# Reordering the head of a fused FFT and maxout feed-forward kernel

## The chip, the cores and the metric

The kernel runs on one core of one Trainium2 chip. The metric is the device time of one execution in microseconds (us), as the median over runs. A profiled execution also has a span, from its first to its last profiled instruction; the span is a little shorter than that execution's own time.

## The reference

The input x is 8 batches of 3072 rows by 256 columns. Each batch gets a two-dimensional Fourier transform, of which only the real part is kept. Then a feed-forward layer with three weight matrices and a maximum runs over all 24576 rows.

```python
def _attn_ref(x):
    X = np.fft.fft(x, axis=1)
    X = np.fft.fft(X, axis=2)
    return X.real.astype(np.float32)

def _moe_ref(x, w1, w2, w3, w_out):            # d_model 256, d_ff 768
    h = np.maximum(np.maximum(x @ w1, x @ w2), x @ w3)
    return (h @ w_out).astype(np.float32)
```

## The kernel before

**The work.** The transform over the 256 columns is folded into the weights. The kernel multiplies a cosine table `md` (and its negative `nmd`) with the differences of the weights and keeps the results as `g_all`, six blocks of 128 columns of the hidden layer; `gd_all` holds, scaled by one number per partition, those halves of `g_all` that belong to the odd part. `g1t` and `gw` are further products of the weights. What is left per batch is the transform over 3072 rows, in two steps, into an even part `tE` and an odd part `tO`, each 128 x 1536, and then the feed-forward layer on them. By symmetry each matmul pair gives a row k and its mirror 3072 - k: `hp` is the hidden layer of the one, `hm` of the other.

**Units.** A batch has 18 units: three blocks of 512 columns of `tE` and `tO`, times six blocks of the hidden layer. The loop over units at the end of the kernel writes the order of the work out by hand, and each engine executes in that order. A unit is `begin` (the plus matmuls L490 and L491, a relu on ACT into `stmp` L503, a maximum on DVE into `hp` L504) and, one unit later, `finish` (the minus matmuls L497 onto the same banks, the same relu and maximum into `hm`). From unit 7 on, every second unit takes its third term in another way (L814 to L844). The output matmuls of a block (L513, L536) are spread over the six units behind it.

**The head.** Everything ahead of the unit loop prepares batch 0. This report calls it the head, and units 0 to 5 the first block.

- GpSimd (POOL) makes index ramps (`iota`, L150), issues the loads of x (L127, four chunks of slots in two halves each) and of the weights (`load_w`, L173, in columns 0 to 128, 128 to 384 and 384 to 768), and later the loads of batch 1.
- DVE makes small per-partition numbers (`scal` L213, `mad` L217), the angles `vm` and `kvec`, and the mirrored half of each chunk of x (`mirror` L134); the mirrored first column goes to ACT or DVE (L138).
- PE multiplies each chunk with a table (`Mix.s`, L401 and L411, s(0) to s(6)), with matmuls on zeros in between (`warm_up`, L640). ACT or DVE copies the result from PSUM to `tb` (L408, L416). DVE transposes `tb` to `yb` in one instruction (`Mix.t`, L434), and `Mix.k` (L466) multiplies `yb` with the tables `te_tab` and `to_tab` that ACT makes (`table`, L302 to L306). `k(0, g)` gives block g of `tE`, `k(1, g)` block g of `tO`.
- `products` (L314) multiplies tables and weights into a PSUM bank, and `keep` (L328) copies the bank to `g_all`; `psg0` is hidden block 0, `psg1` and `psg2` are the two parts of blocks 1 and 2. `differ` (L335) makes `gd_all` from `g_all`.

**PSUM.** The head has two rings of banks: `ps_f`, three banks that last through the whole kernel, and `ps_s`, five banks that are closed ahead of the unit loop. The space of `ps_s` then becomes the banks of the units (`pse2`, `pse3`, `po`).

**Work placed among the units.** `plan` lists what batch 0 does behind `begin` of each unit: `m.c` (copies single columns into `yb`, L459), `m.f` (fills the edge rows of `yb`, L438 and L440), `m.k` for the later blocks, `angle` and `table` for the last third of the angles, and the generators `prep_first` (four pieces for hidden blocks 3 to 5, L314 and L344) and `prep_second` (`g1t`, L370 and L374; then `gw`, L379 and L384).

Of the kernel before, what the change touches and what calls it, by code (L numbers as in the profile page):

```python
# [51 lines left out]
def kernel(  # L52
# [9 lines left out]
    nc = tc.nc  # L62
# [9 lines left out]
    RI = 17  # L72
# [6 lines left out]
    ps_f = ctx.enter_context(tc.tile_pool(name="ps_f", bufs=3, space=bass.MemoryType.PSUM))  # L79
# [8 lines left out]
    tbw = tb.rearrange("p (f s) -> p f s", s=32)  # L88
# [56 lines left out]
    gen = ctx.enter_context(tc.tile_pool(name="gen", bufs=1))  # L145
    ps_s_cm = tc.tile_pool(name="ps_s", bufs=5, space=bass.MemoryType.PSUM)
    ps_s = ps_s_cm.__enter__()

    def iota(t, pattern, base=0, cm=0):
        nc.gpsimd.iota(t, pattern, base=base, channel_multiplier=cm,  # L150
                       allow_small_or_imprecise_dtypes=True)
# [2 lines left out]

    pidx = gen.tile([128, 1], FP32, tag="pidx")
    iota(pidx, [[0, 1]], cm=1)
    NA = 32 + 2 * RI
    ang_r = gen.tile([128, NA], FP32, tag="ang_r")
    iota(ang_r[:, 0:32], [[0, 2], [1, 16]], base=1)
# [11 lines left out]
    def load_w(k, j0, j1):  # L171
        wsrc, wdst = ((moe_w1, w1_bf), (moe_w2, w2_bf), (moe_w3, w3_bf))[k]
        nc.gpsimd.dma_start(  # L173
            out=wdst.rearrange("p (fc j) -> p fc j", fc=2)[:, :, j0:j1],
            in_=wsrc.rearrange("(fc p) j -> p fc j", fc=2)[:, :, j0:j1])
# [10 lines left out]
    load_w(1, 0, 128)  # L186
    ramp(6)
    load_w(2, 0, 128)
    for k in range(3):
        load_w(k, 128, 384)  # L190
    ramp(11)
# [10 lines left out]
    nc.vector.memset(half_pi, 0.5 * math.pi)  # L202
    ang_o = gen.tile([128, NA], FP32, tag="ang_o")
    nc.vector.memset(ang_o, 0.0)
    nc.vector.memset(ang_o[:, 15:32], 8.0)
    nc.vector.memset(ang_o[:, NA - RI:NA], 24.0)
    nc.vector.memset(ang_r[:, 31:32], 0.0)
# [23 lines left out]
    mad(ang_r, ang_r, alpha, ang_o)  # L231
    _reduce(nc, ang_r, ang_r, ang_q, 32.0)
    nc.scalar.activation(out=ang_q, in_=ang_r, func=AX.Sin, scale=float(2.0 * math.pi / 32.0))
    half = gen.tile([128, 256], FP32, tag="half")
    nc.vector.memset(half[:, 0:128], 64.0)
    nc.vector.memset(half[:, 128:256], 0.0)
    par = gen.tile([128, 2], FP32, tag="par")
    scal(par[:, 1:2], pidx, 0.5, ALU.mult, -0.25, ALU.add)
    scal(par[:, 1:2], par[:, 1:2], ROUND, ALU.add)
    scal(par[:, 1:2], par[:, 1:2], -ROUND, ALU.add, -2.0, ALU.mult)  # L240
    nc.vector.tensor_tensor(out=par[:, 1:2], in0=par[:, 1:2], in1=pidx, op=ALU.add)
    scal(par[:, 1:2], par[:, 1:2], 64.0, ALU.mult)
    scal(par[:, 0:1], par[:, 1:2], -1.0, ALU.mult, 64.0, ALU.add)
    nc.vector.tensor_copy(out=tab[:, 0:64:2], in_=ang_q[:, 0:32])
    scal(tab[:, 1:64:2], ang_q[:, 0:32], sig, ALU.mult)
    scal(tabx, ang_q[:, 32:NA], sgm, ALU.mult)
# [2 lines left out]
    vm = gen.tile([128, 512], FP32, tag="vm")  # L249
    qm = gen.tile([128, 512], FP32, tag="qm")  # L250
    pf = gen.tile([128, 2], FP32, tag="pf")
    rnd = gen.tile([128, 2], FP32, tag="rnd")
    for fc in range(2):
        scal(pf[:, fc:fc + 1], pidx, float(128 * fc), ALU.add)
        nc.vector.scalar_tensor_tensor(
            out=vm[:, fc * 256:(fc + 1) * 256].rearrange("p (k c) -> p k c", c=128),
            in0=dvec.unsqueeze(1).to_broadcast([128, 2, 128]), scalar=pf[:, fc:fc + 1],
            in1=half.rearrange("p (k c) -> p k c", c=128), op0=ALU.mult, op1=ALU.add)
    nc.vector.memset(rnd[:, 0:1], ROUND)
    nc.vector.memset(rnd[:, 1:2], -ROUND)  # L260

    def turns(q, v, per):

# [20 lines left out]
    mad(vm, qm, -256.0, vm)  # L284
    nc.vector.tensor_copy(out=vm.rearrange("p (fc k c) -> p fc k c", fc=2, k=2)[:, :, :, 0],
                          in_=par.unsqueeze(1).to_broadcast([128, 2, 2]))
    nc.vector.memset(tbw[:, :, 24:32], 0)
    mirror(0, *FIRST[1])

    def angle(part, c0=1024, c1=NHALF + 1):  # L290
        cs = slice(c0, c1)
        if part == 0:
            phase(c0, c1)
            scal(q[:, cs], kvec[:, cs], 1.0 / 3072.0, ALU.mult, ROUND, ALU.add)
        else:
            scal(q[:, cs], q[:, cs], -ROUND, ALU.add, -3072.0, ALU.mult)
            nc.vector.tensor_tensor(out=kvec[:, cs], in0=kvec[:, cs], in1=q[:, cs], op=ALU.add)

    def table(k, c0=1024, c1=NHALF + 1):
# [18 lines left out]
    def products(pool, i0, i1, j0, j1, tag="ps"):  # L318

        psg = pool.tile([128, 512], FP32, name="psg", tag=tag)  # L320
        for i in range(i0, i1):
            for half in range(2):
                product(psg, (2 * (i - i0) + half) * (j1 - j0), i, half, j0, j1)
        return psg

    def keep(psg, i0, i1, j0, j1, evict):

        evict(out=g_all[:, j0 // 128:j1 // 128, 2 * i0:2 * i1, :],  # L328
              in_=psg[:, 0:2 * (i1 - i0) * (j1 - j0)].rearrange("p (k c j) -> p c k j", j=128,
                                                               c=(j1 - j0) // 128))  # L330

    def differ(i0, i1, j0, j1):

        cs = slice(j0 // 128, j1 // 128)
        nc.vector.tensor_scalar(out=gd_all[:, cs, i0:i1, :], in0=g_all[:, cs, 2 * i0 + 1:2 * i1:2, :],  # L335
                                scalar1=dif, scalar2=None, op0=ALU.mult)
# [51 lines left out]
    class Mix:  # L388
# [46 lines left out]

        def f(self):
            for a in (0, 64):
                nc.scalar.copy(out=ybv[a + 32:a + 64, 0], in_=ybv[a:a + 32, 16])  # L438
                for r in (0, 32):
                    nc.vector.memset(ybw[a:a + 32, r:r + 2, :], 0)  # L440

        def col(self, slot, which):
            return ybv[:, (slot + 1) % RI, which, :]
# [194 lines left out]
    def warm_up(n):  # L638
        for _ in range(n):
            nc.tensor.matmul(warm, zero[:, 0:128], zero, start=True, stop=True)  # L640

    m = Mix(0)
    warm_up(17)
    m.s(0, pool=ps_s)
    m.s(1, pool=ps_s)
    warm_up(5)
    wrap(0, 512)
    mirror(0, *FIRST[2])
    nc.scalar.activation(out=md_all, in_=vm, func=AX.Sin, scale=float(2.0 * math.pi / 256.0))
    m.s(2, pool=ps_s)  # L650
    m.s(3, pool=ps_s)
    phase(512, 1024)
    mirror(0, *FIRST[3])
    m.s(4, pool=ps_s)
    scal(sgn, pidx, 0.0, ALU.is_equal)
    scal(sgn, sgn, 2.0, ALU.mult, -1.0, ALU.add)
    m.s(5, pool=ps_s, evict=dve)
    m.s(6, pool=ps_s)
    m.t()
    nc.scalar.activation(out=nmd_all, in_=vm, func=AX.Sin, scale=float(-2.0 * math.pi / 256.0))  # L660
    table(0, 0, 512)
    table(1, 0, 512)
    table(2, 0, 512)
    for k in range(3):
        load_w(k, 384, 768)
    m.u()
# [9 lines left out]
                                in_=moe_w_out.rearrange("(jc p) c -> p jc c", jc=NJC))  # L676
    psg0 = products(ps_f, 0, 2, 0, 128)
    keep(psg0, 0, 2, 0, 128, nc.scalar.copy)
    psg1 = products(ps_s, 0, 1, 128, 384)
    m.x0(x0s)  # L680
    warm_up(2)
    m.c(1, 7)
    m.k(0, 0, dve)
    m.k(1, 0)
    psg2 = products(ps_s, 1, 2, 128, 384)
    wrap(512, 1024)
    keep(psg1, 0, 1, 128, 384, dve)
    scal(dif, sgn, 1.0, ALU.subtract)
    differ(0, 2, 0, 128)
    keep(psg2, 1, 2, 128, 384, dve)  # L690
    table(1, 512, 1024)

    rows_f = gen.tile([128, 12 * B], FP32, tag="rows_f")
    iota(rows_f.rearrange("p (b t u) -> p b t u", t=4, u=3), [[S, B], [-4, 4], [-1025, 3]],
# [5 lines left out]
    pool = nc.gpsimd  # L700
# [60 lines left out]
        mirror(b, *EIGHTHS[ch])  # L761

    for (u, fn) in ((0, lambda: table(2, 512, 1024)), (0, lambda: m.c(7, 16)),
                    (0, lambda: next(second)), (0, lambda: differ(0, 2, 128, 384)),
                    (1, lambda: table(0, 512, 1024)), (2, m.f), (2, lambda: m.c(0, 1)),
                    (2, lambda: m.c(16, RI)),
                    (1, lambda: m.k(1, 1)), (1, lambda: next(second)), (1, lambda: angle(0)),
                    (2, lambda: m.v(1)), (2, lambda: m.k(0, 1)),
                    (2, lambda: next(first)), (2, lambda: next(first)), (2, lambda: next(second)),
                    (2, lambda: next(first)), (2, lambda: next(first)), (2, lambda: angle(1)),  # L770
                    (3, lambda: table(1)), (3, lambda: table(2)), (3, lambda: table(0)),
                    (4, lambda: m.k(1, 2)), (4, lambda: m.k(0, 2)), (4, m.end),
                    (5, column), (5, lambda: next(second)), (6, lambda: m.v(2))):
        at(0, u, fn)
# [145 lines left out]
```

## Time and profile before

| | |
|---|---|
| median of 3 runs | 403.43 us (403.2 to 405.6) |
| profiled execution, own time | 403.34 us |
| its span | 401.5 us |
| mean granted TensorE clock | 0.989 |
| PE matmul busy | 383.7 us (96%), 2755 matmuls |
| DVE busy | 321.0 us (80%), 542 instructions |
| ACT busy | 262.6 us (65%), 476 instructions |
| POOL busy | 329.9 us (82%), 422 instructions |
| HBM read and written | 36.95 MB and 30.81 MB |

An engine's busy time is the time in which it has an instruction under way. A busy share over the whole span is a mean over stages; the head and the first block, some 43 us, differ from the other 350 us. The granted clock is the share of full speed that TensorE runs at. A line of a timeline has the start in us, the duration, the engine, the line of the kernel and the tiles; in brackets the idle time of the engine ahead of it, and what ended it.

### The profile page before, as it was taken

How to read it: one execution, taken by the hardware profiler on the slowest of the kernel's cores; microseconds unless marked ns; L12 is line 12 of the kernel's file. 1: busy time of each engine (PE TensorE's matmuls, PEld its weight loads, DVE VectorE, ACT ScalarE, POOL GpSimd, SP SyncE). 2: the span in 40 equal slices, each digit the busy share in tenths (PEclk: the TensorE clock that was granted, in tenths of full speed). 3: DMA queues.
4: the chain of work that ended last, by engine and by line, in shares of the span. 5: the costliest groups of instructions: out<-in, count | busy, mean ns of one | idle time of the engine just before them, and what ended most of it. 6: DMA issues, size and time to landing. Idle time of an engine off the chain costs nothing.

```text
span 401.5 us, 8422 instructions
## 1 busy us (share of the span) xinstructions
PE 383.7 (96%) x2755; PEld 237.7 (59%) x2755; DVE 321.0 (80%) x542; ACT 262.6 (65%) x476; POOL 329.9 (82%) x422
## 2 busy tenths in 40 slices
PE   6777999999999999999999999999999999999994
PEld 2443555656665566656665666656665666666673
DVE  7877796877887887877887887877887887887982
ACT  3857678768875778668865778568866546544420
POOL 9991279788998899888998899898978798778993
PEclk9799999999999999999999999999999999999999
DMA  8999259386766958495665968396332653322234
GB/s 115 165 182 175 42 141 196 104 149 182 156 127 132 201 133 154 124 170 157 159 147 111 194 145 165 107 183 169 105 107 83 142 144 100 93 74 53 89 90 133
DMA packets 66901, 54.20 MB, mean 135 GB/s; under 512 B 32702, under 2 KB 62556, under 8 KB 66003
## 3 DMA queue, kind: packets, MB, share of 16 engines
q0 software_dynamic: 24368, 26.53, 35.1%
q1 hardware_dynamic: 41978, 26.72, 26.3%
q8 instruction: 21, 0.34, 0.4%
q10 hardware_dynamic: 512, 0.43, 0.4%
q14 instruction: 22, 0.18, 0.2%
HBM read 36.95 MB, written 30.81 MB: 169 GB/s over the span
## 4 chain that ended last, share of the span: by engine, by line
PE 89%; DVE 5%; ACT 3%; issue 1%; DVEq 0%; ACTq 0%
PE po L513 31%; PE pse L497 12%; PE pse L490 8%; PE pse L491 8%; PE po L536 5%; PE pse L830 4%; PE pse L831 4%; PE e L814 4%; PE d L816 4%; PE ps L401 3%; PE ps L466 3%; PE pl L528 2%; PE psg L314 1%; ACT stmp L503 1%; DVE hp L504 1%
## 5 line engine op out<-in xcount | busy, mean ns | idle before, releaser
L503 ACT ACTIVATE stmp<-pse 128x512 bf16<-128x512 f32 x150 | 89.6, 600 | 66.2 <-PE pse L497 42.0
L823 POOL TENSOR_TENSOR plus<-even,odd 128x512 bf16<-128x512 f32 x69 | 87.8, 1272 | 44.6 <-DVE even L819 27.9
L622 POOL DMA_INDIRECT out_dram<-ot,rows_m x92 | 102.3, 1112 | 17.8 <-issue 9.5
L823 POOL TENSOR_TENSOR minus<-even,odd 128x512 bf16<-128x512 f32 x69 | 87.5, 1269 | 0.0
L513 PE MATMUL po<-wout_bf,hp 128*128 128x256 bf16 x576 | 86.1, 273 | 0.0
L832 DVE SCALAR_TENSOR_TENSOR hp<-pse,plus 128x512 bf16<-128x512 f32 x69 | 47.6, 690 | 43.7 <-PE pse L831 25.2
L513 PE MATMUL po<-wout_bf,hm 128*128 128x256 bf16 x576 | 78.6, 273 | 0.0
L513 PEld LDWEIGHTS <-hp 128*128 128x128 bf16 x576 | 56.3, 98 | 26.1
L497 PE MATMUL pse<-tO,gd_all 128*128 128x512 bf16 x219 | 70.8, 379 | 0.0
L513 PEld LDWEIGHTS <-hm 128*128 128x128 bf16 x576 | 56.4, 98 | 16.3
L541 DVE TENSOR_TENSOR ot<-po,even 128x512 f32<-128x512 f32 x92 | 62.8, 683 | 0.0
L490 PE MATMUL pse<-tE,g_all 128*128 128x512 bf16 x150 | 56.8, 379 | 4.5 <-DVE hm L504 2.1
L504 DVE TENSOR_TENSOR hp<-pse,stmp 128x512 bf16<-128x512 f32 x75 | 51.4, 686 | 10.4 <-ACT stmp L503 9.8
L504 DVE TENSOR_TENSOR hm<-pse,stmp 128x512 bf16<-128x512 f32 x75 | 51.6, 688 | 9.0 <-ACT stmp L503 3.7
L491 PE MATMUL pse<-tO,g_all 128*128 128x512 bf16 x150 | 56.8, 379 | 0.0
L819 DVE SCALAR_TENSOR_TENSOR even<-vb,wcol,e 128x512 f32<-128x512 bf16 x69 | 50.9, 738 | 0.0
L844 DVE SCALAR_TENSOR_TENSOR hm<-pse,minus 128x512 bf16<-128x512 f32 x69 | 47.2, 684 | 2.1 <-PE pse L491 1.5
L818 ACT ACTIVATE odd<-d 128x512 f32<-128x512 f32 x69 | 41.3, 599 | 6.0
L134 ACT COPY xt<-xt 64x762 bf16<-64x762 bf16 (+1 forms) x48 | 40.2, 838 | 1.1
L536 PE MATMUL po<-gw,tO 128*128 128x512 bf16 x92 | 34.9, 380 | 0.0
L497 PEld LDWEIGHTS <-gd_all 128*128 128x128 bf16 x219 | 21.3, 97 | 23.1 <-issue 5.0
L405 ACT CAST tb<-ps 128x512 bf16<-128x512 f32 x40 | 21.6, 588 | 14.8 <-PE ps L401 14.0
(177 smaller groups left out, 488.9 us busy)
## 6 DMA issues: line engine op xcount, KB each, us to landing
xt<-in_x_dram POOLq DMA_DIRECT2D x14, 384.0 KB
out_dram<-ot SPq DMA_DIRECT2D x55, 96.0 KB
out_dram<-ot SPq DMA_DIRECT2D x64, 64.0 KB
db<-tb SPq DMA_DIRECT2D x21, 192.0 KB
vb<-vd SPq DMA_DIRECT2D x23, 128.0 KB
xt<-in_x_dram POOLq DMA_DIRECT2D x7, 400.0 KB
xt<-in_x_dram POOLq DMA_DIRECT2D x7, 368.0 KB
out_dram<-ot SPq DMA_DIRECT2D x62, 32.0 KB
```

The costliest lines, as they stand in the source:

```text
L490: nc.tensor.matmul(pse[:, 0:n], g_all[:, jc, 2 * i, :], te, start=True, stop=False)
L491: nc.tensor.matmul(pse[:, 0:n], g_all[:, jc, 2 * i + 1, :], to, start=False, stop=True)
L497: nc.tensor.matmul(pse, gd_all[:, jc, i, :], to, start=False, stop=True, skip_group_check=True)
L503: nc.scalar.activation(out=stmp[:, 0:n], in_=pses[0][:, 0:n], func=AX.Relu)
L504: nc.vector.tensor_tensor(out=dst, in0=src3, in1=stmp[:, 0:n], op=ALU.max)
L513: nc.tensor.matmul(po, hcols(jc), wout_bf[:, jc * 256:(jc + 1) * 256], start=False, stop=(jc == NJC - 1), skip_group_check=True)
L536: nc.tensor.matmul(po, to[:, cp], gw[:, 256:768], start=True, stop=True)
L541: nc.vector.tensor_tensor(out=ot.rearrange("p (h c) -> p h c", h=2), in0=po.rearrange("p (h c) -> p h c", h=2), in1=lin.unsqueeze(1).to_br ...
L622: stored(nc.gpsimd.indirect_dma_start(out, bass.IndirectOffsetOnAxis(ap=rows_m[0:128 - lo, at_row: at_row + 1], axis=0), ot[lo:128, 256:51 ...
L819: nc.vector.scalar_tensor_tensor(out=even3, in0=vb, scalar=wcol[:, jc:jc + 1], in1=e3, op0=ALU.mult, op1=ALU.add)
L823: nc.gpsimd.tensor_tensor(out=dst, in0=even3, in1=odd3, op=op)
L832: nc.vector.scalar_tensor_tensor(out=dst, in0=pse2, scalar=0.0, in1=sums[g][0], op0=ALU.max, op1=ALU.max)
```

## The change

It touches the head and the plan of units 0 to 3 of batch 0. The rest of the kernel is the same text.

- Small numbers on DVE: the parity of the partition (`par`) comes from an integer ramp and a bit operation, three instructions in place of six; the tile `half` and its two memsets go, and `vm` is made by four `tensor_scalar` in place of two `scalar_tensor_tensor`; the two memsets of `rnd` move to the front. One `iota` is added on POOL ahead of the loads.
- The memset of the spare slots of `tb` moves from DVE to POOL, between two loads of weights.
- `phase(512, 1024)` moves on DVE from behind the third mirror to ahead of the second.
- s(3) is copied by DVE in place of ACT, s(5) by ACT in place of DVE, s(6) by DVE in place of ACT.
- Fillers: 18 + 4 + 1 + 2 + 2 + 3 = 30 matmuls on zeros in place of 17 + 5 + 2 = 24.
- `psg1` and `psg2` go from the ring `ps_s` to the ring `ps_f`; `psg1` is copied by ACT ahead of `m.k`, in place of DVE behind it. ACT makes `table(1)` and `table(2)` behind the copy of `psg0`.
- `differ(0, 2, 128, 384)` and `m.f` move from units 0 and 2 into the head, and `m.f` from ACT and DVE to POOL, ahead of the row numbers (`rows_f`) and of POOL's mirrors of batch 1.
- The plan: one piece of `prep_first` goes behind unit 0 and one behind unit 1, two stay at unit 2 (before, all four were there); `table(0, 512, 1024)` comes later in unit 1; the last two `m.c` go to unit 3.

```diff
     iota(pidx, [[0, 1]], cm=1)
+    pidx_i = gen.tile([128, 1], INT32, tag="pidx_i")
+    nc.gpsimd.iota(pidx_i, [[0, 1]], base=0, channel_multiplier=1)
...
     load_w(2, 0, 128)
+    nc.gpsimd.memset(tbw[:, :, 24:32], 0)
     for k in range(3):
         load_w(k, 128, 384)
...
+    rnd = gen.tile([128, 2], FP32, tag="rnd")
+    nc.vector.memset(rnd[:, 0:1], ROUND)
+    nc.vector.memset(rnd[:, 1:2], -ROUND)
...
-    half = gen.tile([128, 256], FP32, tag="half")
-    nc.vector.memset(half[:, 0:128], 64.0)
-    nc.vector.memset(half[:, 128:256], 0.0)
     par = gen.tile([128, 2], FP32, tag="par")
-    scal(par[:, 1:2], pidx, 0.5, ALU.mult, -0.25, ALU.add)
-    scal(par[:, 1:2], par[:, 1:2], ROUND, ALU.add)
-    scal(par[:, 1:2], par[:, 1:2], -ROUND, ALU.add, -2.0, ALU.mult)
-    nc.vector.tensor_tensor(out=par[:, 1:2], in0=par[:, 1:2], in1=pidx, op=ALU.add)
-    scal(par[:, 1:2], par[:, 1:2], 64.0, ALU.mult)
-    scal(par[:, 0:1], par[:, 1:2], -1.0, ALU.mult, 64.0, ALU.add)
+    odd = gen.tile([128, 1], INT32, tag="odd")
+    nc.vector.tensor_scalar(out=odd, in0=pidx_i, scalar1=1, scalar2=None, op0=ALU.bitwise_and)
+    scal(par[:, 1:2], odd, 64.0, ALU.mult)
+    scal(par[:, 0:1], odd, -64.0, ALU.mult, 64.0, ALU.add)
...
-        nc.vector.scalar_tensor_tensor(
-            out=vm[:, fc * 256:(fc + 1) * 256].rearrange("p (k c) -> p k c", c=128),
-            in0=dvec.unsqueeze(1).to_broadcast([128, 2, 128]), scalar=pf[:, fc:fc + 1],
-            in1=half.rearrange("p (k c) -> p k c", c=128), op0=ALU.mult, op1=ALU.add)
-    nc.vector.memset(rnd[:, 0:1], ROUND)
-    nc.vector.memset(rnd[:, 1:2], -ROUND)
+        for k, c in ((0, 64.0), (1, 0.0)):
+            scal(vm[:, (2 * fc + k) * 128:(2 * fc + k + 1) * 128], dvec, pf[:, fc:fc + 1], ALU.mult,
+                 c, ALU.add)
...
-    nc.vector.memset(tbw[:, :, 24:32], 0)
+    phase(512, 1024)
     mirror(0, *FIRST[1])
...
         def f(self):
             for a in (0, 64):
-                nc.scalar.copy(out=ybv[a + 32:a + 64, 0], in_=ybv[a:a + 32, 16])
+                nc.gpsimd.tensor_copy(ybv[a + 32:a + 64, 0], ybv[a:a + 32, 16])
                 for r in (0, 32):
-                    nc.vector.memset(ybw[a:a + 32, r:r + 2, :], 0)
+                    nc.gpsimd.memset(ybw[a:a + 32, r:r + 2, :], 0)
...
-    warm_up(17)
+    warm_up(18)
     m.s(0, pool=ps_s)
     m.s(1, pool=ps_s)
-    warm_up(5)
+    warm_up(4)
...
     m.s(2, pool=ps_s)
-    m.s(3, pool=ps_s)
-    phase(512, 1024)
+    m.s(3, pool=ps_s, evict=dve)
+    warm_up(1)
     mirror(0, *FIRST[3])
     m.s(4, pool=ps_s)
+    warm_up(2)
...
-    m.s(5, pool=ps_s, evict=dve)
-    m.s(6, pool=ps_s)
+    m.s(5, pool=ps_s)
+    m.s(6, pool=ps_s, evict=dve)
     m.t()
+    warm_up(2)
     nc.scalar.activation(out=nmd_all, in_=vm, func=AX.Sin, scale=float(-2.0 * math.pi / 256.0))
     table(0, 0, 512)
-    table(1, 0, 512)
-    table(2, 0, 512)
...
     keep(psg0, 0, 2, 0, 128, nc.scalar.copy)
-    psg1 = products(ps_s, 0, 1, 128, 384)
+    table(1, 0, 512)
+    table(2, 0, 512)
+    psg1 = products(ps_f, 0, 1, 128, 384)
     m.x0(x0s)
-    warm_up(2)
+    keep(psg1, 0, 1, 128, 384, nc.scalar.copy)
+    warm_up(3)
     m.c(1, 7)
     m.k(0, 0, dve)
     m.k(1, 0)
-    psg2 = products(ps_s, 1, 2, 128, 384)
+    psg2 = products(ps_f, 1, 2, 128, 384)
     wrap(512, 1024)
-    keep(psg1, 0, 1, 128, 384, dve)
     scal(dif, sgn, 1.0, ALU.subtract)
     differ(0, 2, 0, 128)
     keep(psg2, 1, 2, 128, 384, dve)
     table(1, 512, 1024)
+    differ(0, 2, 128, 384)
+    m.f()
...
     for (u, fn) in ((0, lambda: table(2, 512, 1024)), (0, lambda: m.c(7, 16)),
-                    (0, lambda: next(second)), (0, lambda: differ(0, 2, 128, 384)),
-                    (1, lambda: table(0, 512, 1024)), (2, m.f), (2, lambda: m.c(0, 1)),
-                    (2, lambda: m.c(16, RI)),
-                    (1, lambda: m.k(1, 1)), (1, lambda: next(second)), (1, lambda: angle(0)),
-                    (2, lambda: m.v(1)), (2, lambda: m.k(0, 1)),
-                    (2, lambda: next(first)), (2, lambda: next(first)), (2, lambda: next(second)),
-                    (2, lambda: next(first)), (2, lambda: next(first)), (2, lambda: angle(1)),
+                    (0, lambda: next(second)), (0, lambda: next(first)),
+                    (1, lambda: m.k(1, 1)), (1, lambda: next(second)), (1, lambda: next(first)),
+                    (1, lambda: table(0, 512, 1024)), (1, lambda: angle(0)),
+                    (2, lambda: m.v(1)), (2, lambda: m.k(0, 1)), (2, lambda: next(first)),
+                    (2, lambda: next(second)), (2, lambda: next(first)), (2, lambda: angle(1)),
+                    (3, lambda: m.c(16, RI)), (3, lambda: m.c(0, 1)),
                     (3, lambda: table(1)), (3, lambda: table(2)), (3, lambda: table(0)),
                     (4, lambda: m.k(1, 2)), (4, lambda: m.k(0, 2)), (4, m.end),
```

More of the change, by code (lines that the diff above doesn't have):

```diff
@@ L251 @@
     pf = gen.tile([128, 2], FP32, tag="pf")
-    rnd = gen.tile([128, 2], FP32, tag="rnd")
     for fc in range(2):
         scal(pf[:, fc:fc + 1], pidx, float(128 * fc), ALU.add)
-        nc.vector.scalar_tensor_tensor(
-            out=vm[:, fc * 256:(fc + 1) * 256].rearrange("p (k c) -> p k c", c=128),
-            in0=dvec.unsqueeze(1).to_broadcast([128, 2, 128]), scalar=pf[:, fc:fc + 1],
-            in1=half.rearrange("p (k c) -> p k c", c=128), op0=ALU.mult, op1=ALU.add)
-    nc.vector.memset(rnd[:, 0:1], ROUND)
-    nc.vector.memset(rnd[:, 1:2], -ROUND)
+        for k, c in ((0, 64.0), (1, 0.0)):
+            scal(vm[:, (2 * fc + k) * 128:(2 * fc + k + 1) * 128], dvec, pf[:, fc:fc + 1], ALU.mult,
+                 c, ALU.add)
     def turns(q, v, per):
```

## The prediction

> **What bounds the kernel now.** I read the page's slices first, then busy time by stage, the waits between 20.9 and 43 us, and the timeline of the head.
>
> In the slices (of 10 us each), PE is short of full only in the first three or four and in the last, and TensorE's clock dips in the second:
>
> ```profile
> PE   6777999999999999999999999999999999999994
> PEclk9799999999999999999999999999999999999999
> ```
>
> Busy time by stage (the stretch, its length, then busy us with the instruction count in brackets for PE, weight loads, DVE, ACT and POOL; then granted clock, DMA share and GB/s):
>
> ```profile
> 10.71:14.13 3.42, 1.75 (x10) 0.39 (x8) 3.28 (x7) 3.32 (x8) 3.35 (x8) 1.00 1.47 188
> 14.13:20.95 6.82, 6.14 (x44) 4.35 (x45) 5.13 (x6) 4.36 (x11) 6.64 (x11) 0.50 1.15 154
> 20.95:24.37 3.42, 1.72 (x14) 1.08 (x12) 2.52 (x6) 1.32 (x3) 3.08 (x8) 1.00 0.96 148
> 24.37:42.84 18.47, 14.41 (x126) 8.34 (x125) 14.22 (x27) 13.16 (x29) 7.17 (x13) 1.00 1.08 166
> 60.00:390.00 330.00, 329.63 (x2391) 206.26 (x2389) 269.57 (x423) 223.50 (x399) 285.62 (x345) 1.00 0.58 135
> ```
>
> From 60 us on PE has no gap (329.63 of 330), so whatever the head gives is kept to the end. The head itself is not PE's: PE idles 1.7 us in 20.95 to 24.37 and 4.06 us from there to 42.84, where batch 1's first s() starts. I take that start as the mark: the change is worth what it moves it. From 14.13 to 20.95 the clock is half.
>
> Waits (who waited for whom; total us, times, longest):
>
> ```profile
> DVE hp L504 <- ACT stmp L503: 3.3, 3, 1.3
> PE pse L490 <- DVE hm L504: 2.1, 2, 1.3
> PE pse L490 <- DVE g_all L328: 1.7, 1, 1.7
> PE pst L370 <- DVE g_all L344: 1.4, 1, 1.4
> ```
>
> In the timeline, the third line's wait is unit 0 waiting for the copy of `psg2`, whose bank it takes over. In the first block DVE sets the pace: `hp` of units 0, 1, 2 and 3 starts at 24.89, 27.46, 30.17 and 36.50.
>
> ```profile
> 10.52 0.48 DVE L287 MEMSET tb<- 128x512 uint32 x1
> 15.73 3.75 DVE L434 STREAM_TRANSPOSE yb<-tb 128x2048 uint32<-128x2048 uint32 x1
> 19.15 1.01 PE L640 MATMUL warm<-zero 128*128 128x512 bf16 x2
> 23.63 0.38 PE L490 MATMUL pse<-tE,g_all 128*128 128x512 bf16 x1 [1.71 <-DVE g_all L328]
> 25.83 1.56 POOL L134 COPY xt<-xt 64x1651 bf16<-64x1651 bf16 x1
> 26.09 1.45 DVE L335 TENSOR_SCALAR gd_all<-g_all,dif 128x512 bf16<-128x512 bf16 x1
> 42.84 0.62 PE L401 MATMUL ps<-xt,tab 128*64 128x512 bf16 x4
> ```
>
> **The change, step by step.** All times are from the span's start.
>
> *Up to the transpose.* DVE works without a gap from 8.14 to 14.57, so its list sets the transpose, until the data does: by the trace's completion events the chunks of x land at 7.39, 10.27, 11.59 and 12.97. The added iota ahead of the loads shifts them by 0.1 (iotas start 0.1 to 0.25 apart). Removed before mirror 0: two memsets (start to start 0.15 and 0.08), three of six `par` steps (0.18 each), two memsets of `rnd` (0.02 and 0.05); `vm` is four pieces in place of two of 0.49 (bounds for a 128x128 piece: the memset's 0.17 and the 66-column step's 0.31; I take 0.2). The bit operation is not in the trace: other one-column steps take 0.10 to 0.22, I take 0.15. Together some 1.0, but mirror 0 then waits for data: 7.55 in place of 8.14; half of the saving is covered by that wait, and so is an error in these small costs. Behind it, `phase` (0.62) takes the place of the memset (0.48): mirror 1 at 10.56 (was 11.04, data at 10.37). The angles' step 0.69, mirror 2 0.44, and the copy of s(3) (0.69) in place of `phase` (0.62) put mirror 3 at 13.2 (was 13.62; data at 13.07). s(5) starts at 13.83, ACT copies it from 14.28 (0.59), DVE copies s(6) (0.26) beside it, and the transpose starts at 14.9 in place of 15.73.
>
> The memset of `tb` on POOL is not in the trace: DVE's 0.48 below, POOL's 480-column iota of 0.98 above; nearest is its 128x512 tensor_scalar of 0.61, which I take. POOL idles 0.49 at that place, waiting for x, so the weights behind it come 0 to 0.5 later, I take 0.1. `psg1`'s weights land at 15.45 and are used behind 16.3: covered.
>
> *Transpose to `k`.* It ends at 18.67. At full clock the products are done by then (16 of 128 columns: 0.041 per 96-column matmul below, 0.107 at half clock above, I take 0.06; 8 of 256 at 0.11; three fillers at 0.22: from 15.5 to 18.0 with the waits), and k(0,0) starts at 18.75 in place of 19.96. Its cover is the 3.75 us of the transpose. At half clock the cover is gone: from 15.65, 14 x 0.107, 8 x 0.214, 0.1, and three fillers at 0.427 end at 20.2, 0.25 later than now.
>
> *To `hp` of unit 0.* Unit 0 no longer takes `psg2`'s bank. At full clock DVE does `tE` (19.18, 0.69), the angles' step, `dif`, `gd_all` of block 0, the copy of `psg2` (20.85 to 21.53) and the moved `differ` (rows: 256 columns 0.29, 384 columns 0.35, so about 0.4 for 512), then `hp` at 22.0. PE's unit 0 (20.5 to 21.5) and ACT's `stmp` (21.1 to 21.7) lie beside it; ACT's copy of `psg1` (0.59) lies under the transpose's end and makes k(1,0) wait to 19.4, beside `tE`. So 22.0 in place of 24.89. At half clock the same steps from 20.9 give 23.65.
>
> *`hp` of unit 0 to `hp` of unit 3.* Now 11.6 us. Left on DVE, start to start: five `hp` and `hm` at 0.6 each, 3.0; three `g1t` 1.85; two `g_all` 1.1; two `gd_all` 0.7; `phase`, two steps of `q` and the sum into `kvec` 2.05: 8.7. Gone are four memsets (0.68), the `differ` of 1.45, and 1.1 of waits for ACT's copies of `prep_first`, whose four pieces stood together at unit 2 (the 1.4 us wait above). Each piece now has a unit's time for its copy.
>
> *Rest.* From `hp` of unit 3 to the mark nothing changes: 6.34. The mark is at 22.0 + 8.7 + 6.3 = 37.0 at full clock, 5.8 earlier; at half clock 38.65, 4.2 earlier.
>
> *POOL.* `m.f` stands ahead of POOL's row numbers and its mirrors of batch 1. Six instructions: POOL's smallest (0.19) below, 1.1; ACT's copies (0.40) and twice DVE's memsets (0.33) above, 2.1; I take 1.6. The mirrors move from 25.83 to about 27.6, ending at 31.0; they are used at 37. The row numbers are used after 50, and batch 2's loads behind them, landing by 41.4 now and by 43.2 then, from 48. SP's queue gets nothing new. But a POOL copy holds DVE's `tensor_scalar` on SBUF data: the `gd_all` line of the timeline shows 1.45 for 0.4 of work, released as the copy ends at 27.39. The Trainium skill (SBUF — State Buffer, section "Who interferes with whom") has it as a rule: whichever issues second is fully blocked until the other ends; the trace agrees, with that 1.45, and by the rule the hold estimated next would be 1.5, to the second copy's end. The second `gd_all` and the second step of `q` fall at 29.3 to 30.1, on the mirrors: one hold, 0 to 1.5, I take 1.2.
>
> Sum: 5.8 - 1.2 = 4.6 against the profiled execution's 403.34 (0.1 below the median): 398.7.
>
> **The rivals.**
>
> 1. *The clock still drops.* What it hangs on is 10.71 to 14.13. PE's busy sum there, 1.75, does not tell: with 1.72 the clock held at 24.37. But s() runs as pairs side by side (four matmuls in 0.62); counted once, that stretch streams 1.2 us (five fillers' rest 0.56, three pairs 0.65), the one that held 1.5. Changed, it has four pairs and three fillers: 1.5, if s(5) starts ahead of 14.13. Near the one that held, but not by much. Time: 4.2 - 1.2 = 3.0, so 400.4; with both `phase` and `q` held too, 401.8. The Trainium skill (TensorE: Matmul & The Clock Gate, Part 1) says that the clock halves after one idle window of about 3.4 us, and that windows run free of the kernel's start. The trace agrees on the step (6.83 is two of 3.41) and on the half; but a window with PE half busy counted as idle here, so the measurement decides against "idle". If windows run free, this rival comes in some runs and not in others, which no run here can yet show.
> 2. *No hold.* DVE's steps slip between POOL's copies: 5.8, so 397.5. For: `phase` and `q` ran at 0.53 and 0.43 beside POOL's load issues. Against: the 1.45.
> 3. *Slower: POOL holds DVE throughout.* With `m.f` on POOL, POOL is busy from 16 to 33, and DVE has nine instructions in it with all operands in SBUF. At 1.1 a hold, four holds eat the half-clock gain of 4.2; five give 404.7. Against: beside POOL's small steps `gd_all` took 0.29. By the rule of the Trainium skill named above all nine would be open to it.
>
> **How the numbers follow.** Forecast 0.45, rival 1 0.33, rival 2 0.13, rival 3 0.09. The range 397.3 to 401.9 holds the first three. A measurement can tell about 1% (4 us: 399.4 and 407.5). Faster by more: four fifths of the forecast, rival 2, a little of rival 1: 0.52. Slower by more: rival 3 with eight holds or so: 0.05. Within: 0.43.
>
> **What would show it.** Transpose near 14.9, k(0,0) near 18.75, `hp` of unit 0 at 22.0 without a wait of unit 0 for `psg2`, unit 3's at 31 to 32, the mark at 38.2, granted clock 1.00 from 14.13 to 20.95, and one `tensor_scalar` of over 1 us near 29. Wrong would be: k(0,0) near 20.2 at a clock of 0.50; several long `tensor_scalar`; new PE waits for the three banks of `ps_f`; or a gap behind 43.

## The result and the profile after

The changed kernel takes 399.45 us (median of 6 runs, 398.77 to 400.43) where the kernel before takes 404.62 (6 runs). The ratio is 0.988, with a 95% interval of 0.985 to 0.990. Measured again on another occasion it took 400.42 (7 runs, 399.48 to 404.23), 0.992 of before (0.989 to 0.9945). There the kernel before took 403.29, and 403.25 to 403.59 beside all later kernels, so its 404.62 is high by about 1.2: by medians the gain is 5.2 us the first time and 2.9 the second. The profiled execution took 398.77 with a span of 396.9, against 403.34 and 401.5.

In the page's slices PE's third digit rises from 7 to 9 and the clock's second from 7 to 9:

```profile
PE   7697999999999999999999999999999999999994
PEclk9999999999999999999999999999999999999999
```

Busy time by stage, with the columns of the prediction:

```profile
10.71:14.13 3.42, 1.88 (x10) 0.49 (x9) 3.28 (x7) 3.32 (x8) 3.32 (x8) 1.00 1.47 181
14.13:20.95 6.82, 4.67 (x51) 3.26 (x52) 5.49 (x8) 4.74 (x12) 6.64 (x10) 1.00 1.04 144
20.95:24.37 3.42, 3.42 (x23) 2.01 (x22) 3.20 (x9) 2.58 (x6) 3.14 (x10) 1.00 0.96 150
24.37:42.84 18.47, 15.84 (x134) 9.15 (x135) 15.01 (x29) 14.05 (x32) 8.54 (x18) 1.00 1.06 170
```

The clock held from 14.13 to 20.95, and PE fills 20.95 to 24.37 (1.72 of 3.42 before). Of the waits shown before, the two of PE for the copies to `g_all` (1.7 and 1.4) are gone. Those left:

```profile
DVE hp L501 <- ACT stmp L500: 2.8, 3, 1.3
PE pse L487 <- DVE hm L501: 1.6, 1, 1.6
```

The timeline (start, duration, engine, line; the lines of tables, products and units are three lower than before, `scal` and `mad` are L219 and L223):

```profile
8.49 0.99 DVE L219 TENSOR_SCALAR kvec<-kvec,s_of,phi 128x512 f32<-128x512 f32 x1
8.62 0.58 POOL L150 IOTA kvec<- 128x480 f32 x1
10.12 0.60 DVE L282 COPY vm<-par 128x4 f32<-128x4 f32 x1
10.14 0.55 POOL L191 MEMSET tb<- 128x512 uint32 x1
16.07 3.78 DVE L431 STREAM_TRANSPOSE yb<-tb 128x2048 uint32<-128x2048 uint32 x1 [0.52 <-ACT tb L405]
21.33 0.38 PE L487 MATMUL pse<-tE,g_all 128*128 128x512 bf16 x1
30.18 0.93 DVE L332 TENSOR_SCALAR gd_all<-g_all,dif 128x384 bf16<-128x384 bf16 x1
38.43 0.62 PE L398 MATMUL ps<-xt,tab 128*64 128x512 bf16 x4
```

The mark (last line) moved from 42.84 to 38.43, by 4.4 of the 4.6 that the span lost. The transpose did not move forward: 16.07 against 15.73. Unit 0 starts without a wait at 21.33 (23.63 before).

### The profile page after: what moved, and what is told of

Read it like the earlier page. It is cut to its first block, busy times and chain, and to the rows that moved or that the text cites. A ratio compares the mean times of both kernels' runs of the same rounds, so it can differ in the third digit from the quotient of the medians.

```text
span 396.9 us, 8384 instructions
## 1 busy us (share of the span) xinstructions
PE 379.8 (96%) x2712; PEld 236.5 (60%) x2761; DVE 319.0 (80%) x534; ACT 261.9 (66%) x474; POOL 331.9 (84%) x430
## 4 chain that ended last, share of the span: by engine, by line
PE 83%; DVE 7%; ACT 4%; issue 3%; POOL 1%; DVEq 0%; POOLq 0%; ACTq 0%
PE po L510 30%; PE pse L494 12%; PE pse L487 8%; PE pse L488 6%; PE po L533 5%; PE pse L830 4%; PE d L816 3%; PE e L814 3%; PE pse L831 3%; PE ps L398 3%; PE ps L463 2%; PE pl L525 2%; ACT tb L402 1%; DVE yb L431 1%; ACT stmp L500 1%
## 5 line engine op out<-in xcount | busy, mean ns | idle before, releaser
L488 PE MATMUL pse<-tO,g_all 128*128 128x512 bf16 x129 | 48.9, 379 | 0.1
L533 PE MATMUL po<-gw,tO 128*128 128x512 bf16 x85 | 32.3, 380 | 0.0
```

Of the source, the lines that this page charges most:

```text
L488: nc.tensor.matmul(pse[:, 0:n], g_all[:, jc, 2 * i + 1, :], to, start=False, stop=True)
L533: nc.tensor.matmul(po, to[:, cp], gw[:, 256:768], start=True, stop=True)
```

## The experiments

Eleven further kernels were run, and the changed one once more, each beside the kernel before on the same chip; the ratio is to those runs (before: 403.25 to 403.59 us in them). All times inside the span come from the profiled execution. "hp0" and "hp3" are the starts of `hp` of units 0 and 3; "half" is how long the granted clock was 0.50 ahead of the mark, after it had first become full (4.9 to 7.6 us into the span; until then the fillers follow each other 0.43 apart, in place of 0.22).

| kernel | us | ratio (95%) | transpose | hp0 | hp0 to hp3 | mark | half |
|---|---|---|---|---|---|---|---|
| before | 404.62 | 1 | 15.73 | 24.89 | 11.61 | 42.84 | 6.83 |
| changed | 399.45 | 0.988 (0.985 to 0.990) | 16.07 | 23.15 | 8.94 | 38.43 | 0 |
| changed, again | 400.42 | 0.992 (0.989 to 0.9945) | 17.60 | 24.75 | 10.42 | 42.11 | 6.83 |
| old banks | 401.40 | 0.996 (0.993 to 0.999) | 16.03 | 23.95 | 11.14 | 41.44 | 0 |
| pieces together | 399.47 | 0.991 (0.988 to 0.994) | 15.71 | 22.72 | 10.23 | 39.29 | 0 |
| old fillers | 400.50 | 0.994 (0.992 to 0.996) | 16.22 | 23.29 | 9.99 | 39.62 | 3.41 |
| old copies | 399.95 | 0.991 (0.988 to 0.9945) | 15.82 | 22.95 | 9.58 | 40.16 | 3.41 |
| m.f back | 401.65 | 0.995 (0.9925 to 0.998) | 16.24 | 23.25 | 11.72 | 42.69 | 6.83 |
| vm in two steps | 399.87 | 0.990 (0.988 to 0.993) | 16.17 | 23.25 | 8.94 | 38.53 | 0 |
| fillers alone | 404.66 | 1.003 (1.001 to 1.005) | 15.58 | 24.08 | 12.43 | 42.85 | 0 |
| head alone | 404.15 | 1.002 (1.000 to 1.004) | 17.23 | 26.95 | 11.74 | 45.03 | 10.24 |
| tail alone | 399.95 | 0.990 (0.988 to 0.992) | 15.93 | 23.59 | 9.22 | 40.45 | 10.24 |
| angles on POOL | 398.38 | 0.988 (0.985 to 0.991) | 16.12 | 23.34 | 7.33 | 37.70 | 0 |
| best | 397.00 | 0.984 (0.982 to 0.985) | 15.63 | 22.61 | 7.74 | 36.69 | 3.41 |

In all fourteen profiles the span behind the mark is 358.3 to 359.1 us. So nearly the whole difference lies ahead of the mark. One profile explains one execution, not the median.

### Old banks

```diff
-    psg1 = products(ps_f, 0, 1, 128, 384)
+    psg1 = products(ps_s, 0, 1, 128, 384)
-    psg2 = products(ps_f, 1, 2, 128, 384)
+    psg2 = products(ps_s, 1, 2, 128, 384)
```

> The changed kernel (399.45 us, mark at 38.43 us from the span's start) with psg1 and psg2 back in the short-lived ring ps_s. Theory: unit 0's first plus matmul again waits for the copy of psg2 (22.00 to 22.68 on DVE), so it starts near 22.75 in place of 21.33, hp of unit 0 near 24.3 in place of 23.15, and the mark comes 1.2 later: 400.6 us. Rival: DVE sets the pace of the whole block and does the next unit's copies during the wait, so that at most 0.5 is lost: 399.5 to 399.9 us.

The wait is back as foretold: unit 0's first matmul starts at 22.69, after a wait of 1.25 for the copy of `psg2`. `hp` of unit 0 comes 0.8 later, not 1.2. The mark, however, comes 3.0 later. Most of the other 2.2 are two DVE steps that met POOL's mirrors: `gd_all` took 1.50 and `phase` 1.76, where they take 0.34 and 0.53 undisturbed. The wait for the bank is shown; the price of it differs with what the shifted steps meet.

### Pieces together

```diff
-(0, next(first)), (1, next(first)), (2, next(first)), (2, next(first))
+(2, next(first)), (2, next(first)), (2, next(first)), (2, next(first))
```

> The changed kernel with the order of units 0 to 2 as before: all four pieces of prep_first together at unit 2, and the table of block 1 ahead of the products at unit 1 (m.f and differ stay where the change put them). Theory: the four pieces want a bank of ps_f each in a row, PE waits for their copies (1.4 us in one wait before the change), and hp of unit 0 to hp of unit 3 takes 10.0 to 10.5 us in place of 8.94: 400.6 to 401 us. Rival: the saving between these two came from the memsets and the differ that left DVE, not from the spread: 9.0 us there, 399.4 to 399.7 us.

The excerpt shows the pieces alone; `table(0, 512, 1024)` and the last two `m.c` also went back to their old places, so the run tests the old order of units 0 to 2 as a whole. Both are half right. hp0 to hp3 takes 10.23, as the theory says, with PE waiting 0.6 and DVE 0.6 for the copies. But that profile's transpose came 0.36 earlier, and the medians of this kernel and the changed one can't be told apart. The new order is worth 1.3 us in the profile (POOL held DVE there by 0.7 in both) and was not resolved in the times.

### Old fillers

```diff
-    warm_up(18) ... warm_up(4) ... warm_up(1) ... warm_up(2) ... warm_up(2) ... warm_up(3)
+    warm_up(17) ... warm_up(5) ... warm_up(2)
```

> The changed kernel with the fillers as before the change (17, 5, none, none, none, 2 in place of 18, 4, 1, 2, 2, 3). Theory: the stretch 10.71 to 14.13 holds about 1.2 us of PE's streaming again, and the granted clock is 0.50 from 14.13 to 20.95. The products then end near 20.2 in place of 18.2, k(0,0) starts near 20.2 in place of 19.90, psg2's products lie partly in the half clock, hp of unit 0 near 24.0 in place of 23.15: 400.3 us. Rival 1: the transpose hides it all, since k(0,0) waits for it anyway: clock 0.50 and 399.5 us. Rival 2: s() in the new order is enough, the clock stays at 1.00, and 399.3 us.

The clock did drop, for 3.41 us from 15.80, and 400.50 is near the expected 400.3; a good third of the delay is the theory's. The transpose itself came 0.15 later. Behind it, unit 0's first matmul is another 0.47 late. `hp` of unit 0 doesn't feel that, since DVE's list sets it, as rival 1 has it (hp0 is 0.14 later). But the delay stays on PE: unit 1's relu starts 0.62 later, then ACT's copy of a piece (26.71 in place of 26.09), and with it DVE's `gd_all`, at 27.22 in place of 26.60:

```profile
27.22 0.35 DVE L332 TENSOR_SCALAR gd_all<-g_all,dif 128x384 bf16<-128x384 bf16 x1
28.06 1.73 DVE L219 TENSOR_SCALAR q<-kvec 128x513 f32<-128x513 f32 x1
```

The mark is 1.19 late. Of that, 0.15 is the transpose, 0.47 the delay behind it, and 0.57 that POOL held `q` by 1.30 (1.73 in place of 0.43), where the first profile of the changed kernel has holds of 0.73.

### Old copies of s(3), s(5), s(6)

```diff
-    m.s(3, pool=ps_s, evict=dve) ... m.s(5, pool=ps_s) ... m.s(6, pool=ps_s, evict=dve)
+    m.s(3, pool=ps_s) ... m.s(5, pool=ps_s, evict=dve) ... m.s(6, pool=ps_s)
```

> The changed kernel with the copies of s(3), s(5) and s(6) back on the engines that had them before (ACT, DVE, ACT in place of DVE, ACT, DVE). Theory: the copy of s(3) on DVE (0.69) ahead of the last mirror, and the way from ACT's copy of s(5) to DVE's transpose (0.34 from end to start), are why the transpose came 0.34 later than before and not 0.83 earlier. Without them the last mirror is at 13.2, the transpose at 15.2 to 15.3 in place of 16.07, k(0,0) at 19.1, and the mark 0.8 earlier: 398.65 us. Rival: behind the transpose ACT sets the pace (its copy of psg1, then c(1,7), then the copy for tO), these move by 0.3 at most, and the time is 399.1 us.

The transpose came at 15.82, 0.25 earlier and not 0.8. The way from the last copy to the transpose is 0.10 again in place of 0.34, as the theory has it. The rest of it was not tested: with the copy of s(3) gone, DVE idled 0.70 ahead of the last mirror, waiting for x, whose last rows landed at 13.80 in this run, but at 13.18 in the first profile of the changed kernel (12.97 to 13.80 in all fourteen, by the trace's completion events). The time is not better. A sum of DVE's list held (1.82 in place of 0.70) left PE 1.14 us of work in a window of 3.41, and the clock was half in the next:

```profile
31.32:34.73 3.41, 1.14 (x7) 0.39 (x5) 2.49 (x3) 2.05 (x4) 3.41 (x6) 1.00 0.61 101
34.73:38.14 3.41, 3.41 (x25) 1.78 (x24) 1.80 (x3) 2.58 (x7) 0.52 (x1) 0.50 0.91 143
```

### The changed kernel, again

> The changed kernel once more, unaltered. Theory: two things in its first 40 us are not set by the code but by where POOL and the clock happen to stand. The same head has put the transpose at 15.71, 16.03, 16.07 and 16.22 in four kernels that share it, and POOL's mirrors have held one DVE step of hp of unit 0 to hp of unit 3 by 0.6 to 1.3 us, in one kernel two steps by 2.4. So the transpose comes anywhere between 15.7 and 16.2, hp of unit 0 to hp of unit 3 takes anything from 8.4 to 10.5, and the profiled execution 398.3 to 400.5 us. Rival: the first profile is what the code gives: 16.07, 8.94 and 398.8, each within 0.1 or 0.2.

The theory holds, and its bounds were too narrow: the transpose came at 17.60, hp0 to hp3 took 10.42, the profiled execution 402.6. Three things of this execution:

```profile
6.03 1.19 DVE L219 TENSOR_SCALAR vm<-dvec,pf 128x128 f32<-128x128 f32 x1
6.39 0.78 POOL L175 DMA_DIRECT2D w_bf<-in_moe_w_dram  x1
29.45 1.76 DVE L219 TENSOR_SCALAR kvec<-kvec,s_of,phi 128x513 f32<-128x513 f32 x1
29.48 1.45 POOL L134 COPY xt<-xt 64x1524 bf16<-64x1524 bf16 x1
```

A piece of `vm` ends as POOL's issue of a load ends, at 7.2, 0.9 late; the first mirror then starts at 8.45 in place of 7.66 and everything up to the transpose follows. Later two steps, `gd_all` and `phase`, wait for POOL's mirrors. The clock dropped twice, behind windows with 1.48 and 1.07 us of PE's work. The first cost nothing: k(0,0) starts 0.06 after the late transpose ends. The second lengthened the way from hp3 to the mark from 6.34 to 6.94.

### `vm` in two steps

```diff
-        for k, c in ((0, 64.0), (1, 0.0)):
-            scal(vm[:, (2 * fc + k) * 128:(2 * fc + k + 1) * 128], dvec, pf[:, fc:fc + 1], ...)
+        nc.vector.scalar_tensor_tensor(out=vm[...], in0=dvec..., scalar=pf[:, fc:fc + 1], in1=half..., ...)
```

> The changed kernel with vm built as before, in two steps that read two tensors (scalar_tensor_tensor, 0.48 and 0.49 in the profile of before), in place of four tensor_scalar pieces of one; the constants they add are set early, where DVE waits. Theory: DVE steps that read one SBUF tensor are held by POOL's iota and by its issue of loads, steps that read two are not. In the second profile of the changed kernel one piece of vm took 1.19, in two others the pieces ended with POOL's iota or load issue 0.7 to 1.2 late, and everything behind came late with them (transpose at 17.60 and 17.23). With two-tensor steps the first mirror starts at 7.3 to 7.8 in every run, the transpose at 15.6 to 16.2, and no run is above 401 us: 399.2 us with a spread of 398.5 to 400.5. Rival: the late head has nothing to do with the form of vm; the spread stays at 398.8 to 404 us and the median at 399.5 to 400.4.

Two constant halves (`half`) return with it, which the excerpt leaves out. The point on the form is shown: the two-tensor step runs beside POOL's issue of a load (6.41 to 7.19) and is not held, as in the profile of before, where it took 0.48 from 7.28 inside an iota. The mirror behind it, a copy, is held, by the iota from 7.15 to 7.87:

```profile
6.42 0.48 DVE L258 SCALAR_TENSOR_TENSOR vm<-dvec,pf,half 128x256 f32<-128x256 f32 x1
7.26 1.16 DVE L134 COPY xt<-xt 64x2032 bf16<-64x2032 bf16 x1
```

But nothing was won: the mirror, 0.4 earlier, met the iota and took 1.16 in place of 0.81, and the transpose is at 16.17. The time is 399.87, not 399.2. That no run was above 401 us (6 runs; 2 of 13 of the changed kernel were) fits the theory and is too little to prove it.

### Parts alone

"Fillers alone" puts the change's `warm_up` counts into the kernel before:

> The kernel before with one part of the change alone: its fillers (18, 4, 1, 2, 2, 3 in place of 17, 5, none, none, none, 2). Theory: the granted clock stays at 1.00 from 14.13 to 20.95, and since the transpose hides most of that stretch and unit 0 still waits for the copy of psg2 behind DVE's list, only 0.4 us come of it: 402.9 us where the kernel before has 403.3. Rival 1: the clock is worth what the prediction put on it, 1.6 us: 401.7 us. Rival 2: with s(3) and s(5) in the old order a window still falls short, the clock drops, and nothing is gained.

The clock held, hp0 came 8.50 behind the transpose in place of 9.16 and 0.81 earlier in all, and yet hp3 came at 36.51, where it was 36.50: DVE's next steps ran into POOL's mirrors (`phase` 1.13, `q` 1.70). So the clock is worth 0.66 up to hp0, and alone it gains nothing. Why the median is even 0.3% above before is open: the profiled execution (403.09) is one of the shorter of its ten, and what the longer ones meet was not seen.

"Head alone" puts everything up to the transpose, without fillers, into the kernel before:

> The kernel before with another part alone: all that the change does to DVE's, ACT's and POOL's lists up to the transpose (fewer small sums, the four pieces of vm, POOL's memset of tb, the phase step moved ahead, the copies of s(3), s(5) and s(6)), with fillers, banks, products and m.f as before. Theory: what is saved ahead of the first mirror is spent again, on the copy of s(3) in DVE's list, on DVE steps that now meet POOL's iota and memset, and on the way from ACT's copy of s(5) to the transpose: the transpose comes at 15.7 to 16.2 (15.73 before) and the time is 403.2 to 403.6 us. Rival: the first profile of the changed kernel was an unlucky one, the transpose comes at 14.9 to 15.2, and the time is 402.5 us.

The theory's sign is right: this part gains nothing. The transpose at 17.23 is outside its range, by the same hold of `vm` as above (1.20).

"Tail alone" puts everything behind the transpose into the kernel before, without the new fillers:

> The kernel before with only what the change does behind the transpose: psg1 and psg2 in ps_f, the copy of psg1 on ACT, differ and m.f (on POOL) ahead of unit 0, the products spread over units 0 to 2; DVE's list up to the transpose and the fillers as before. Theory: this part alone makes the gain: unit 0 does not wait for the copy of psg2, DVE loses four memsets and a held differ, hp of unit 0 comes near 23.8 and hp of unit 3 near 33: 400.0 to 400.5 us where the kernel before has 403.3. Rival: the parts need each other, since at half clock the products end late and POOL's mirrors meet other DVE steps; 402 us or more.

As far as the intervals tell, this is the change's whole gain: 0.990, though this profile has 10.24 us at half clock. Unit 0 has no wait, hp0 is at 23.59, and hp0 to hp3 takes 9.22. Half clock did cost something: k(0,0) starts 4.23 behind the transpose's start, as in the kernel before (3.81 with the fillers alone), and hp0 comes 7.66 behind it, where the first profile of the changed kernel has 7.08.

### `m.f` back on ACT and DVE

```diff
-                nc.gpsimd.tensor_copy(ybv[a + 32:a + 64, 0], ybv[a:a + 32, 16])
+                nc.scalar.copy(out=ybv[a + 32:a + 64, 0], in_=ybv[a:a + 32, 16])
-                    nc.gpsimd.memset(ybw[a:a + 32, r:r + 2, :], 0)
+                    nc.vector.memset(ybw[a:a + 32, r:r + 2, :], 0)
...
-    m.f()
+ (2, m.f)
```

> The changed kernel with m.f back where it was: its two copies on ACT (0.40 each) and its four memsets on DVE (0.68 together) at unit 2, in place of POOL ahead of unit 0. Theory: DVE's 0.68 come back between hp of unit 0 and hp of unit 3, and POOL, free 1.7 earlier, starts its mirrors as soon as batch 1's rows land, near 26.5 in place of 27.8, so that they meet the first group of DVE's SBUF steps (gd_all, phase, q at 26.6 to 28.0) and hold it by 1.2 to 1.9 in place of the second by 0.6. hp of unit 0 to hp of unit 3 takes 10.5 to 11 in place of 8.94, and the time is 400.6 to 401.2 us. Rival: the hold only changes its place and stays at 0.6, and 0.7 us are all that m.f is worth: 400.0 us.

The theory is right, with more than it expected: hp0 to hp3 takes 11.72, the time is 401.65. POOL's mirrors start as x lands, at 27.05, and each holds a step from its first to its last moment:

```profile
27.05 1.84 DVE L219 TENSOR_SCALAR kvec<-kvec,s_of,phi 128x513 f32<-128x513 f32 x1
27.05 1.56 POOL L134 COPY xt<-xt 64x1651 bf16<-64x1651 bf16 x1 [1.00 <-DMA xt<-in_x_dram]
28.89 1.45 POOL L134 COPY xt<-xt 64x1524 bf16<-64x1524 bf16 x1
28.93 1.70 DVE L219 TENSOR_SCALAR q<-kvec 128x513 f32<-128x513 f32 x1
```

In this profile the two holds are 2.6 together, 1.9 more than in the first profile of the changed kernel. So `m.f` on POOL is worth more for what it delays on POOL than for the 0.68 that it takes from DVE.

### The angles on POOL, and the best version

The angle steps that the mirrors hold go to POOL, which runs them one after the other with its mirrors:

```diff
+    phase(1024, NHALF + 1)                    # DVE, ahead of the copy of s(6)
...
     m.f()
+    scal(qa, ka, 1.0 / 3072.0, ALU.mult, ROUND, ALU.add, eng=nc.gpsimd)
+    scal(qa, qa, -ROUND, ALU.add, -3072.0, ALU.mult, eng=nc.gpsimd)
+    nc.gpsimd.tensor_tensor(out=ka, in0=ka, in1=qa, op=ALU.add)
+    mirror(1, 0, 13)
+    mirror(1, 13, 25)
+    load_x(2, ...)                            # four loads, ahead of the row numbers
...
-(1, lambda: angle(0)) ... (2, lambda: angle(1))
```

> The changed kernel with DVE's last three steps for batch 0's angles (two of q, the sum into kvec: 0.43, 0.41 and 0.70 in the last profile) given to POOL behind m.f, the phase step in front of them put ahead of the copy of s(6), where DVE waits, POOL's two mirrors of batch 1 and the loads of batch 2 ahead of POOL's row numbers. Theory: it is the meeting of POOL's mirrors with these DVE steps on SBUF that costs 0.6 to 2.4 us in units 0 to 3 and differs from run to run. Without them no DVE step there takes over 1 us, hp of unit 0 to hp of unit 3 takes 8.0 to 8.5 (PE's own work there is 8), the mark comes near 37.8, and the time is 398.4 us with a smaller spread. Rival: POOL's three steps are themselves held by DVE or hold it, kvec comes late for the table at unit 3, and the time is 399.5 to 400.5 us.

The time is as the theory has it: 398.38, with the mark at 37.70. Its reason is not shown. One `gd_all` was still held:

```profile
26.79 1.44 DVE L332 TENSOR_SCALAR gd_all<-g_all,dif 128x384 bf16<-128x384 bf16 x1
26.53 1.55 POOL L134 COPY xt<-xt 64x1651 bf16<-64x1651 bf16 x1
```

That is a hold of 1.1, more than the 0.73 in the first profile of the changed kernel. hp0 to hp3 fell from 8.94 to 7.33 all the same, below the 8.0 expected, because the four angle steps, 2.1 us there from start to start, are gone from DVE's list in that stretch. So here the gain is work that left DVE; what the missing meetings are worth was not separated from it. The runs lie within 1.2 us (4 runs), but those of the pieces together, whose angle steps are on DVE, lie within 0.8 (4 runs). The way from hp3 to the mark grew to 7.03, since ACT had no gap there; the last kernel takes that up:

```diff
+ vm in two steps, and the old copies of s(3), s(5), s(6), as above
-    scal(sgn, ...)                            # ahead of the transpose
     m.t()
+    scal(sgn, ...)
...
-(3, lambda: table(1))
+(2, lambda: table(1))                         # behind m.k(0, 1)
```

> The kernel with the angle steps on POOL (398.4 us) with four more edits: vm in two-tensor steps as before the change, the copies of s(3), s(5) and s(6) back on ACT, DVE and ACT, the two steps of sgn behind the transpose, and the first of ACT's three last tables (q from kvec) at unit 2, where ACT waits 0.9, in place of unit 3, where ACT was busy from 30.8 to 35.8 without a gap. Theory: the transpose comes at 15.6, hp of unit 3 near 30.3, unit 4 no longer waits 0.5 for ACT's stmp, the mark is at 36.7 in place of 37.70: 397.3 us. Rival: x's last rows and PE's own work set the pace, and it is 398.2 to 398.6 us.

It met the theory: transpose 15.63, hp3 at 30.35, mark 36.69, and 397.00 us, 1.6% under before and in every run under every run of the changed kernel. It did so with one window at half clock, from 13.59 to 17.00.

## Why the prediction was right, and where it was not

The forecast was 398.7 with a gain of 4.6 in the span; the first profile has a gain of 4.6, the second of the same kernel 0.8. The two medians, 399.45 and 400.42, both lie inside the range. The steps, by the first profile:

- **Up to the transpose: wrong.** Forecast 0.83 earlier, measured 0.34 later. The first mirror came at 7.66 (7.55 forecast), the second at 11.01 (10.56), the last at 13.87 (13.2), the transpose at 16.07 (14.9). The step that failed is the sum on DVE's list up to the transpose: it takes most steps at the time that they had at their old places. Being earlier, `phase` met more of the iota (0.99 in place of 0.71); the copy into `vm` met POOL's memset of `tb`, which the prediction priced (0.61; it took 0.55) without the hold on DVE (0.60 in place of 0.17); the second mirror took 0.94 in place of 0.72 and the copy of the last first column 0.36 in place of 0.17; and s(5)'s copy on ACT ends 0.34 ahead of the transpose, where DVE's own ended 0.10 ahead. x was not the limit in this profile: its last rows landed at 13.18. Alone this part gained nothing.
- **Transpose to `k`: right.** 3.83 from one start to the other, 3.85 forecast.
- **`k` to `hp` of unit 0: right.** 3.25 as forecast, without unit 0's wait; the old banks brought it back.
- **hp0 to hp3: right in kind, 1.0 too long.** 8.94 against 9.9. The hold was there, on `gd_all` at 30.18 (0.93, so 0.6) and 0.15 on `phase`, not 1.2. The rest is 8.2 and not 8.7, because the sum has most steps longer than they take from start to start: three `g1t` 1.77 (1.85), two `g_all` 0.94 (1.1), two `gd_all` 0.55 without the hold (0.7), the angle steps 1.96 (2.05).
- **Rest: right.** 6.34 from hp3 to the mark, and 6.34 or 6.35 in each of the changed kernel's variants without a clock drop there, unless ACT's list was changed. Where the clock dropped there it took 6.94 to 7.72.
- **POOL: right.** `m.f` took 1.69 (1.6), the mirrors ran from 27.82 to 31.15 (27.6 to 31.0).

So the total was right by luck: two errors cancel, 1.2 too hopeful ahead of the transpose and 1.0 too careful behind `hp` of unit 0. What it had right in kind lies behind the transpose, and the tail alone shows that this part makes the gain.

**Rival 1** (the clock drops) came in the changed kernel's second profile and in others, and it had the place right but the price too high. 1.65 was put on the way to hp0. From the transpose to hp0 it took 7.15 in the second profile and 7.07 with the old fillers, each with one window at half clock, against 7.08 at full clock; with two windows, in tail alone, 7.66. The transpose and DVE's list cover the most of it, though with the old fillers 0.47 came through later, at unit 1. Its open question is settled: the windows run free of the kernel's start. Counted back in steps of 3.41 us from the first change of clock, they begin 0.47 us behind the span's start in the profile of before, 0.54 in the first after, 0.80 in the second, 2.15 with the old fillers and 3.35 in the best version. The Trainium skill (TensorE: Matmul & The Clock Gate, Part 1) states this, and the traces agree.

**Rival 2** (no hold) did not come. **Rival 3** (POOL holds DVE throughout) has the right mechanism: one hold of 0.6 in the first profile, two of 1.0 and 1.2 in the second, up to 2.6 together in a variant. Four or five of 1.1 were never seen. What the prediction did not have is that these holds differ from run to run in one and the same kernel, and that they can start a drop of the clock in units 3 and 4.

## What to carry to other kernels

Before counting a saving on an engine's list, look at what its later steps will meet when they come earlier: here 0.8 us (the fillers alone) and 0.4 us (`vm` in two steps) won ahead of a hold were lost in it. Where DVE and POOL work side by side, ask which of DVE's steps can be held and what POOL will be doing then, and move one or the other: `m.f` ahead of the mirrors on POOL was worth more for their later start than for the work that it took from DVE. That putting both sides of a hold on one engine makes the runs steadier is not shown here. One profile of such a head is one draw: take a second before believing a cause smaller than 1 us.

## What the hardware showed that was not expected

**Which DVE steps are held.** In fourteen profiles a `tensor_scalar` or `copy` on SBUF data waited for POOL's iotas, memsets, copies and issue of loads, up to 1.3 us a time. `scalar_tensor_tensor` of two SBUF tensors, which stood beside iotas and load issue nearly always, took 0.69 at most there, and 0.76 the one time that it met a POOL copy. A `tensor_tensor` on two SBUF operands took 1.82 in place of 0.70 beside POOL's copy. The Trainium skill (SBUF — State Buffer, section "Who interferes with whom") has the distinction: a DVE instruction with two SBUF inputs contends with a GpSimd instruction that reads SBUF, and not with one that only writes it. The traces agree: 0.48 beside load issue and iota, 1.82 beside a copy.

**When the clock drops.** Full clock was followed by half clock behind windows of 3.41 us with 1.07 to 1.50 us of PE's work; windows with 1.56 to 1.72 held it:

```profile
11.04:14.45 3.41, 1.48 (x10) 0.31 (x8) 3.25 (x7) 3.28 (x8) 3.34 (x8) 1.00 1.49 181
14.45:17.86 3.41, 3.41 (x12) 0.90 (x13) 2.17 (x7) 2.32 (x6) 3.23 (x7) 0.50 1.14 152
```

```profile
20.75:24.16 3.41, 1.56 (x12) 0.87 (x10) 1.99 (x6) 1.34 (x3) 3.15 (x8) 1.00 0.85 136
24.16:27.57 3.41, 3.10 (x22) 1.65 (x21) 3.41 (x7) 3.28 (x7) 2.19 (x7) 1.00 1.47 217
```

The first pair is the changed kernel's second profile, the other the fillers alone. Two windows do not fit, 1.75 in the profile of before and 1.83 in that of the best version, and both dropped; both lie over s(2) to s(4), whose matmuls run in pairs side by side. That pairs count once, as the prediction supposed, fits. Count what PE streams in each full-clock window of the fourteen profiles, at 0.216 us per 512 columns (the spacing of the units' matmuls) and a pair once: these two have 1.21 and 1.25, no other window that dropped has more than 1.23 but one (1.31, in head alone), and those that held have 1.29 or more (up to 46 us into the span). It is an estimate with a thin margin, and no run tried it by itself. The window ahead of the transpose in the first profile of the changed kernel has 1.31 by this count, not the 1.5 of rival 1, since s(5) started behind it, at 14.69: that its clock held was close.
